# Attention keys of a block in one row, one score product per head; the guard of eight weight parts moved to the end

## The chip, the cores and the metric

The kernel runs on one core of a Trainium2 chip. The metric is device time in microseconds (us) of that core; the median of 3 runs of the kernel before is 688.71 us (688.39 to 688.76). Five engines run side by side, each through its own list of instructions in order: TensorE (PE; its weight loads are shown as PEld), VectorE (DVE), ScalarE (ACT), GpSimd (POOL) and SyncE (SP), which here issues all loads and stores. They wait for each other through semaphores.

## The reference

Attention with a band and a few global keys, and two feed-forward layers ("MoE" in the code) behind it:

```python
scores = scale * np.matmul(q, k.transpose(0, 1, 3, 2))     # 2 x 8 heads, 768 tokens, 64 per head
keep = is_global | is_local            # column < 8, or 0 <= row - column < 96
scores = scores + bias[None, :, :, :]  # -slope of the head * distance
scores = np.where(keep, scores, -1000000000.0)
a = softmax(scores)
x = np.matmul(a, v)                    # 1536 tokens x 512
h = np.maximum(x @ w_in, 0.0)          # 512 -> 2048
x = h * h @ w_out                      # -> 512
gate = 1.0 / (1.0 + np.exp(-(x @ w_gate)))
out = gate * (x @ w_val) @ w_out2      # 512 -> 1536 -> 512
```

The MoE weights arrive as 64-bit floats, 68 parts of 128 x 512 numbers. A kernel decodes them to 32-bit floats with integer operations on the two 32-bit halves of each number, and splits each into a high and a low half for products of better precision.

## The kernel before, in words

`_fast` describes the whole work as tasks for a planner (`_Plan`): engine, estimated duration, rank, and the buffers read and written. `issue` lets the tasks run in a model of the engines, by rank among those that are ready, and writes them out in that order, which then is the order of each engine's instructions. Estimated durations thus set only the order.

**Attention.** The 1536 tokens are 12 blocks of 128 queries (`bt`, six for each batch; `t` is the block's number in its batch). A block sees its own 128 keys, the last 96 of the block before (columns 32 to 127), and the first 32 keys of the batch. `rows_of` (L432) loads keys `k` and queries `q` with two DMAs each, one for each group of heads; at the first block of a batch two more bring the first 32 columns, `kf`. Three key buffers and two query buffers are there. Each block has two halves of four heads. `scores` (L467) makes a half's products: for each of two head pairs and both heads, one product against own keys and, after the first block, one against `kf` (32 columns) and one against the 96 columns of the block before, which lie in that block's key buffer:

```python
parts = [(k_t, slice(0, P), 1, 0)]
if t:
    parts = [(kf, slice(0, GS), 0, 0), (ks[bt - 1], slice(GS, P), 0, GS)] + parts
```

Then VectorE adds the bias and takes the minimum (L486), ScalarE takes the exponential (L491), VectorE or ScalarE divides (L510, L512), TensorE transposes (L523, tile `at`), one of the two copies (`ats`, L253 on ScalarE, L255 on VectorE), and TensorE multiplies with the values (L535, tile `o`), which becomes `x` (L543 on).

**MoE.** `moe1` and `moe2` go over the tokens in four passes each, every pass with a quarter of the weights. A `step` (L608) is three products (L615 to L617). The first pass of `moe1` has groups of 256 tokens and runs between the attention blocks; from some 157 us there are only MoE products. 80 small products on zeros (L397) fill TensorE where nothing else is ready, and 8 more (L393) open the program.

**Weights.** `load_weight` (L567) handles one part: a load `wst` (L576, two buffers); ScalarE's absolute value of the high word into `wu` (L583); VectorE's maximum with a smallest number (L585), which keeps numbers too small for the format from being misread; two shifts (L587); "or" with the low word's top bits (L589); "or" with sign and top exponent bit (L592); ScalarE's copy to the high half (L253); VectorE's difference as the low half (L263).

**A second path.** `gen_i` is set from the two sizes given at run time (`whether`, L373). At the end all engines read it, and where it isn't zero they run `_general`, which is not run here.

Of the kernel before, what the change touches and what calls it, by code (L numbers as in the profile page):

```python
# [9 lines left out]
F32 = mybir.dt.float32  # L10
# [7 lines left out]
P = 128  # L18
# [6 lines left out]
F64_MIN = 2.0 ** -15 * 1.125  # L25


@with_exitstack
def kernel(
# [16 lines left out]
    pers = ctx.enter_context(tc.tile_pool(name="pers", bufs=1))  # L46
    nf = pers.tile([P, 2], F32, name="nf")
# [3 lines left out]
    with tc.tile_pool(name="sb", bufs=1) as sb, tc.manual_schedule():  # L51
        _fast(tc, sb, qw, kw, vw, nums, w1, w2, out, nf, gen_i, ident, slopes)
# [160 lines left out]
def _fast(tc, sb, qw, kw, vw, nums, w1, w2, out, nf, gen_i, ident, slopes):  # L213
# [31 lines left out]
    def dma(size):  # L245
        return max(620, size / 350.0)
# [30 lines left out]
    consts = buf("sb", [P, 1], F32, "consts")  # L277
    ni = buf("early", [P, 2, 2], I32, "ni")
# [11 lines left out]
    def setup():  # L290
# [82 lines left out]
        def whether():  # L373
# [9 lines left out]
            v.tensor_copy(gen_i, ok)  # L383

        add("dve", 1300, 1e8, whether, r=[num], w=[(consts, "gen"), (small, "ok")])
# [25 lines left out]
    ks = {}  # L411
# [8 lines left out]
    for bt in range(NQ):  # L420
# [20 lines left out]
        add("sp", 2 * dma(P * NH2 * P * 2), rank_att(i0) - 8900, rows_of(q_t, qw[bt]), w=[q_t],  # L441
            late=2000)
        if t == 0:
            kf = buf("early", [P, NH2, GS], F32, "kf", 2)
            add("sp", 1300, rank_att(i0) - 4000, rows_of(kf, kw[bt], slice(0, GS)), w=[kf],
                late=2000)
# [10 lines left out]
        for half in both:  # L457
# [5 lines left out]
            parts = [(k_t, slice(0, P), 1, 0)]  # L463
            if t:
                parts = [(kf, slice(0, GS), 0, 0), (ks[bt - 1], slice(GS, P), 0, GS)] + parts

            def scores(pts=pts, q_t=q_t, parts=parts, half=half):  # L467
# [303 lines left out]
    for n in range(len(chunks)):  # L771
        load_weight(n, when[n])
# [232 lines left out]
```

## Time and profile before

| | before |
|---|---|
| median of 3 runs | 688.71 us |
| the profiled execution | 689.12 us |
| its span, first to last instruction | 687.2 us |
| TensorE busy in the span | 667.9 us, 97% |
| VectorE | 432.1 us, 63% |
| ScalarE | 285.7 us, 42% |
| mean granted TensorE clock | 0.985 of 2.4 GHz |

The span is what the hardware profiler saw between the first and the last instruction; the execution's own time has 1.9 us around it. A record of a product lasts longer than the distance to the next one, since products are pipelined: distances between starts tell what one costs. "Idle before" of an engine names what ended its idle time. A product on plain 32-bit floats (`k`, `q`, `vv`) shows as two records, a MoE product as one.

### The profile page before, as it was taken

What the parts mean: (1) busy time and instruction counts of PE and PEld (TensorE: products, weight loads), DVE (VectorE), ACT (ScalarE), POOL (GpSimd) and SP (SyncE); (2) the same over time, 40 slices, a digit from 0 to 9 for tenths busy, and PEclk for the clock granted to TensorE, in tenths of its full rate; (3) what the DMA queues carried; (4) which work ended last, traced back from release to release, by engine and by line L of the source; (5) the groups of instructions that cost most, each with busy time, mean ns of one, the idle gap of its engine ahead of it and who ended that gap; (6) DMA issues with size and microseconds to landing.
All of it is one profiled execution on the core that took longest, in us unless ns stands there. A gap on an engine that the chain in (4) does not pass through costs nothing.

```text
span 687.2 us, 10016 instructions
## 1 busy us (share of the span) xinstructions
PE 667.9 (97%) x3864; PEld 558.7 (81%) x3864; DVE 432.1 (63%) x976; ACT 285.7 (42%) x622; POOL 1.1 (0%) x8
## 2 busy tenths in 40 slices
PE   9878999999999999999999999999999999999996
PEld 7766899899988888888888888888888888888884
DVE  5878876768888888888857852476348223222232
ACT  5767777764463444554434541352113111211110
POOL 0000000000000000000000000000000000000000
PEclk9988899999999999999999999999999999999999
DMA  7754433201332332333210230043001000001011
GB/s 181 171 153 139 150 114 107 73 3 63 123 122 78 107 123 87 98 96 119 82 41 32 93 122 1 31 126 120 0 1 62 1 1 0 1 0 62 0 62 66
DMA packets 29335, 51.71 MB, mean 75 GB/s; under 512 B 3808, under 2 KB 16352, under 8 KB 29280
## 3 DMA queue, kind: packets, MB, share of 16 engines
q1 hardware_dynamic: 29280, 51.00, 24.4%
q8 instruction: 32, 0.52, 0.3%
q14 instruction: 23, 0.19, 0.1%
HBM read 47.84 MB, written 3.15 MB: 74 GB/s over the span
## 4 chain that ended last, share of the span: by engine, by line


## 5 line engine op out<-in xcount | busy, mean ns | idle before, releaser
L615 PE MATMUL h<-x,w 128*128 128x512 f32 (+1 forms) x528 | 197.8, 375 | 0.0
L617 PE MATMUL h<-x,w 128*128 128x512 f32 (+1 forms) x528 | 195.7, 371 | 0.0
L616 PE MATMUL h<-x,w 128*128 128x512 f32 (+1 forms) x528 | 195.7, 371 | 0.0
L615 PEld LDWEIGHTS h<-x,w 128*128 128x128 f32 x528 | 99.9, 189 | 17.5 <-issue 0.2
L617 PEld LDWEIGHTS h<-x,w 128*128 128x128 f32 x528 | 99.9, 189 | 16.9
L616 PEld LDWEIGHTS h<-x,w 128*128 128x128 f32 x528 | 100.0, 189 | 16.7
L713 DVE TENSOR_TENSOR r<-h,r 128x512 f32<-128x512 f32 x36 | 24.9, 691 | 103.1 <-PE h L617 101.6
L615 PE MATMUL y<-g,w 128*128 128x512 f32 (+1 forms) x240 | 86.3, 360 | 2.6 <-ACT w L253 1.7
L616 PE MATMUL y<-g,w 128*128 128x512 f32 (+1 forms) x240 | 84.3, 351 | 0.0
L617 PE MATMUL y<-g,w 128*128 128x512 f32 (+1 forms) x240 | 84.3, 351 | 0.0
L263 DVE TENSOR_TENSOR g<-r,g 128x512 fp32r<-128x512 f32 x84 | 57.7, 687 | 17.2 <-ACT g L253 16.7
L710 ACT ACTIVATE r<-h 128x512 f32<-128x512 f32 x36 | 21.5, 598 | 109.7 <-PE h L617 109.6
L583 ACT ACTIVATE wu<-wst 128x512 f32<-128x512 f32 x68 | 45.2, 665 | 48.5 <-DMA wst<-in_w_dram 41.1
L263 DVE TENSOR_TENSOR w<-wx,w 128x512 fp32r<-128x512 f32 x68 | 46.5, 685 | 21.2 <-ACT w L253 20.7
L615 PE MATMUL o<-w,g 128*128 128x512 f32 x144 | 56.9, 395 | 0.0
L616 PE MATMUL o<-w,g 128*128 128x512 f32 x144 | 56.9, 395 | 0.0
L617 PE MATMUL o<-w,g 128*128 128x512 f32 x144 | 56.8, 394 | 0.0
L253 ACT ACTIVATE w<-wx 128x512 fp32r<-128x512 f32 x68 | 42.5, 626 | 34.0 <-DVE wx L592 28.9
L253 ACT ACTIVATE g<-r 128x512 fp32r<-128x512 f32 x32 | 20.2, 632 | 82.5 <-DVE r L713 82.5
L615 PEld LDWEIGHTS y<-g,w 128*128 128x128 f32 x240 | 45.6, 190 | 10.5 <-ACT w L253 2.0
L617 PEld LDWEIGHTS y<-g,w 128*128 128x128 f32 x240 | 45.7, 190 | 6.7 <-DVE w L263 0.2
L616 PEld LDWEIGHTS y<-g,w 128*128 128x128 f32 x240 | 45.7, 191 | 6.4
(79 smaller groups left out, 827.5 us busy)
## 6 DMA issues: line engine op xcount, KB each, us to landing
wst<-in_w_dram SPq DMA_DIRECT2D x68, 512.0 KB, 3.5
k<-in_kw_dram SPq DMA_DIRECT2D x24, 128.0 KB, 2.9
q<-in_qw_dram SPq DMA_DIRECT2D x24, 128.0 KB, 3.1
vv<-in_vw_dram SPq DMA_DIRECT2D x12, 256.0 KB, 2.9
out_dram<-oacc SPq DMA_DIRECT2D x11, 256.0 KB, 2.1
vv<-in_vw_dram SPq DMA_DIRECT2D x10, 192.0 KB, 3.4
vv<-in_vw_dram SPq DMA_DIRECT2D x10, 64.0 KB, 2.8
out_dram<-oacc SPq DMA_DIRECT2D x2, 128.0 KB, 3.6
```

Source lines behind the costliest of these rows:

```text
L253: nc.scalar.activation(to(), of(), ACTF.Copy)
L263: nc.vector.tensor_tensor(to(), of(), less(), op=ALU.subtract)
L583: add("act", act(TN), rank, lambda: nc.scalar.activation(u.ap, hi().bitcast(F32), ACTF.Abs), r=[st], w=[u])
L615: nc.tensor.matmul(p, lhsT=ww[:, 0, ws], rhs=lo, start=first, stop=False)
L616: nc.tensor.matmul(p, lhsT=ww[:, 0, ws], rhs=hi, start=False, stop=False)
L617: nc.tensor.matmul(p, lhsT=ww[:, 1, ws], rhs=hi, start=False, stop=last)
L710: add("act", act(TN), rk, lambda r=r, pt=pt: nc.scalar.activation(r.ap, pt.ap, ACTF.Sigmoid), r=[pt], w=[r])
L713: add("dve", dve(TN), rk, lambda r=r, pt=pt: v.tensor_tensor(r.ap, pt.ap, r.ap, op=ALU.mult), r=[pt], w=[r])
```

## The change

**Keys in one row.** `k` becomes 4 x 2 x 128 numbers per partition: own keys in one window, and in the other, ahead of it, the first 32 keys and the 96 of the block before. The loads write these windows, six DMAs for a block after the first (128, 96 and 32 columns for each group of heads); `kf` and the use of the neighbour's buffer are gone. `scores` makes one product of 256 columns for a head (128 in the first block).

**Guard.** The first eight parts (`TINY = 8`) are decoded with no absolute value and no maximum. All parts take sign and top bit first and add the low word into a new buffer `wf`; the high half is copied from the number without the low word. After the last decode the first eight parts are loaded again, `look_through` counts numbers below the bound, `decide` sums the counts on one partition through a small DMA and sets `gen_i` from them and from the sizes.

```diff
+TINY = 8
...
+    asked = pers.tile([1, P * TINY + 1], F32, name="asked")
...
-        k_t = ks[bt] = buf("early", [P, NH2, P], F32, "k", NQK)
-        def rows_of(to, of, cols=slice(0, P)):
-            def fn():
-                for j in both:
-                    d = slice(j * D, j * D + D)
-                    nc.sync.dma_start(out=to.ap[d], in_=of[d, j::2, cols])
-            return fn
-        add("sp", 2 * dma(P * NH2 * P * 2), rank_att(i0) - 9000, rows_of(k_t, kw[bt]), w=[k_t],
-            late=2000)
...
-            add("sp", 1300, rank_att(i0) - 4000, rows_of(kf, kw[bt], slice(0, GS)), w=[kf],
-                late=2000)
+        k_t = buf("early", [P, NH2, 2, P], F32, "k", NQK)
+        def rows_of(parts):
+            for j in both:
+                d = slice(j * D, j * D + D)
+                for to, of, cols in parts():
+                    nc.sync.dma_start(out=to[d], in_=of[d, j::2, cols])
+        def windows(k_t=k_t, bt=bt, t=t):
+            own, ahead = k_t[:, :, 1], k_t[:, :, 0]
+            parts = [(own, kw[bt], slice(0, P))]
+            if t:
+                parts += [(ahead[:, :, GS:], kw[bt - 1], slice(GS, P)),
+                          (ahead[:, :, 0:GS], kw[bt - t], slice(0, GS))]
+            return parts
+        add("sp", (2 if t == 0 else 4) * dma(P * NH2 * P * 2), rank_att(i0) - 9000,
+            lambda windows=windows, rows_of=rows_of: rows_of(windows), w=[k_t], late=2000)
...
-                    for k, cols, w, c0 in parts:
-                        for j in both:
-                            d = slice(j * D, j * D + D)
-                            nc.tensor.matmul(
-                                pts[j][:, c, w, c0:c0 + cols.stop - cols.start],
-                                lhsT=q_t[d, hp], rhs=k[d, hp, cols], start=True, stop=True)
-            add("pe", 200 + 500 * (2 - lo), rank_att(i), scores, w=pts,
-                r=[q_t] + [k for k, *_ in parts])
+                    for j in both:
+                        d = slice(j * D, j * D + D)
+                        nc.tensor.matmul(pts[j][:, c, lo:], lhsT=q_t[d, hp], rhs=k_t[d, hp, lo:],
+                                         start=True, stop=True)
+            add("pe", 200 + 430 * (2 - lo), rank_att(i), scores, w=pts, r=[q_t, k_t])
...
+        if n < TINY:
+            add("dve", dve(TN, False), rank, lambda: v.tensor_scalar(xi(), hi(), 5, 2, **shift),
+                r=[st], w=[xx])
+        else:
...
-        add("dve", dve(TN), rank, lambda: v.scalar_tensor_tensor(
-            xi(), lo(), 29, xi(), op0=ALU.logical_shift_right, op1=ALU.bitwise_or),
-            r=[st], w=[xx])
         add("dve", dve(TN), rank, lambda: v.scalar_tensor_tensor(
             xi(), hi(), F64_TOP, xi(), op0=ALU.bitwise_and, op1=ALU.bitwise_or), r=[st], w=[xx])
+        full = buf("sb", [P, TN], F32, "wf", 1)
+        add("dve", dve(TN), rank, lambda: v.scalar_tensor_tensor(
+            full.ap.bitcast(I32), lo(), 29, xi(), op0=ALU.logical_shift_right,
+            op1=ALU.bitwise_or), r=[st, xx], w=[full])
         copy(WHI, TN, rank, lambda: t[:, 0], lambda: xx.ap, [xx], [(t, 0)])
-        minus(WLO, TN, rank, lambda: t[:, 1], lambda: xx.ap, lambda: f32(t[:, 0]), [xx, (t, 0)],
-              [(t, 1)])
+        minus(WLO, TN, rank, lambda: t[:, 1], lambda: full.ap, lambda: f32(t[:, 0]),
+              [full, (t, 0)], [(t, 1)])
...
+    def look_through(n):
+        st = buf("sb", [P, TN, 2], I32, "wst", 2)
+        u = buf("sb", [P, TN], F32, "wu", 1)
+        src = w1[chunks[n][1], chunks[n][2]]
+        add("sp", dma(P * TN * 8), 1e7, lambda: nc.sync.dma_start(
+            out=st.ap.rearrange("p n t -> p (n t)"), in_=src), w=[st], late=2000)
+        add("act", act(TN), 1e7, lambda: nc.scalar.activation(
+            u.ap, st[:, :, 1].bitcast(F32), ACTF.Abs), r=[st], w=[u])
+        add("dve", dve(TN) + 80, 1e7, lambda: v.scalar_tensor_tensor(
+            u.ap, u.ap, F64_MIN, u.ap, op0=ALU.is_lt, op1=ALU.mult, accum_out=tiny[:, n:n + 1]),
+            w=[u, (tiny, n)])
+    def decide():
+        add("sp", 700, 1e7, lambda: nc.sync.dma_start(
+            out=asked[:, 0:P * TINY], in_=tiny.ap), r=[(tiny, n) for n in range(TINY)],
+            w=[(consts, "asked")], late=2000)
+        def fn():
+            v.tensor_reduce(asked[:, P * TINY:], asked, axis=AX.X, op=ALU.add)
+            v.tensor_scalar(asked[:, P * TINY:], asked[:, P * TINY:], 0.0, None, op0=ALU.is_gt)
+            v.tensor_copy(gen_i[0:1], asked[:, P * TINY:])
+        add("dve", 1600, 1e7, fn, r=[(tiny, "asked"), (consts, "asked")], w=[(consts, "gen")])
```

The planner's order moves with this. SP, near the start, before: loads of the second block (`k_162`, `q_187`, `vv_210`), of the third (`k_265`, `q_290`) and of the first weight part (`wst_316`).

```order
L436 DMA k_162<-in_kw_dram 64x4x128 x2
L436 DMA q_187<-in_qw_dram 64x4x128 x2
L415 DMA vv_210<-in_vw_dram 128x512
L417 DMA vv_210<-in_vw_dram 32x512
L418 DMA vv_210<-in_vw_dram 96x512
L436 DMA k_265<-in_kw_dram 64x4x128 x2
L436 DMA q_290<-in_qw_dram 64x4x128 x2
L576 DMA wst_316<-in_w_dram 128x1024
```

SP, the same place now, from the second block's queries `q_190` to the first weight part `wst_331`; the six loads of the second block's keys stand just ahead, and look like those of the third, `k_261`.

```order
L440 DMA q_190<-in_qw_dram 64x4x128 x2
L419 DMA vv_214<-in_vw_dram 128x512
L421 DMA vv_214<-in_vw_dram 32x512
L422 DMA vv_214<-in_vw_dram 96x512
L440 DMA k_261<-in_kw_dram 64x4x128
L440 DMA k_261<-in_kw_dram 64x4x96
L440 DMA k_261<-in_kw_dram 64x4x32
L440 DMA k_261<-in_kw_dram 64x4x128
L440 DMA k_261<-in_kw_dram 64x4x96
L440 DMA k_261<-in_kw_dram 64x4x32
L440 DMA q_305<-in_qw_dram 64x4x128 x2
L577 DMA wst_331<-in_w_dram 128x1024
```

Each block's keys take six places instead of two, and the first weight load stands behind twelve key loads of the second and third block, where four and the two of `kf` (ahead of the piece shown) stood.

TensorE, a half of the third block, before: the first six of the 12 products of a half, for the two heads `s_373` and `s_374`.

```order
L473 MATMUL s_373<-kf_138,q_290 128x32
L473 MATMUL s_374<-kf_138,q_290 128x32
L473 MATMUL s_373<-k_162,q_290 128x96
L473 MATMUL s_374<-k_162,q_290 128x96
L473 MATMUL s_373<-k_265,q_290 128x128
L473 MATMUL s_374<-k_265,q_290 128x128
```

TensorE, the same block now: the last two of the four products of the first half, value products and transposes, and the first two of the second half.

```order
L477 MATMUL s_378<-k_261,q_305 128x256
L477 MATMUL s_379<-k_261,q_305 128x256
L537 MATMUL o_334<-ats_351,vv_112 64x128 x2
L537 MATMUL o_334<-ats_375,vv_112 64x128 x2
L525 MATMUL at_411<-ident,sa_311 128x128 x4
L477 MATMUL s_421<-k_261,q_305 128x256
L477 MATMUL s_422<-k_261,q_305 128x256
```

Six products of three widths became two of one width, all from the block's own buffer.

VectorE, decode of the second weight part between the score reductions (`sa`), before: maximum (L585), shift (L587), and the two "or" steps.

```order
L585 TENSOR_SCALAR wx_581<-wu_466 128x512
L486 ISA sa_573,mn_469<-s_450,bias_160 128x256
L486 ISA mn_469 128x1
L587 TENSOR_SCALAR wx_581<-wx_581 128x512
L486 ISA sa_602,mn_603<-s_515,bias_160 128x256
L486 ISA mn_603 128x1
L589 SCALAR_TENSOR_TENSOR wx_581<-wst_391,wx_581 128x512
L497 TENSOR_SCALAR sm_485<-sm_485 128x4
L498 RECIPROCAL sm_485<-sm_485 128x4
L592 SCALAR_TENSOR_TENSOR wx_581<-wst_391,wx_581 128x512
```

VectorE, decode of the second weight part now.

```order
L585 TENSOR_SCALAR wx_552<-wst_430 128x512
L257 COPY ats_561<-at_546 128x512
L596 SCALAR_TENSOR_TENSOR wx_552<-wst_430,wx_552 128x512
L499 TENSOR_SCALAR sm_454<-sm_454 128x4
L500 RECIPROCAL sm_454<-sm_454 128x4
L600 SCALAR_TENSOR_TENSOR wf_584<-wst_430,wx_552 128x512
L514 TENSOR_SCALAR sa_489<-sa_489,sm_454 128x256
L265 TENSOR_TENSOR w_582<-wf_584,w_582 128x512
```

Three steps instead of four, and the first reads the loaded part itself (`wst_430`), not ScalarE's result (`wu_466`); a copy of transposed matrices (`ats_561`) stands between them on VectorE.

## Rows read from the trace of the kernel before

**Rows 1.** Busy time by stages; first the columns, with the mean granted TensorE clock (PEclk).

```profile
core 0: us, PE busy (x) PEld busy (x) DVE busy (x) ACT busy (x) POOL busy (x), PEclk, DMA share, GB/s
20.00:76.50 56.50, 46.18 (x436) 39.25 (x435) 47.37 (x152) 39.35 (x108) 0.00 (x0) 0.85 0.53 149
76.50:157.00 80.50, 80.20 (x869) 72.49 (x867) 58.31 (x210) 57.10 (x172) 0.00 (x0) 1.00 0.27 82
...
400.00:600.00 200.00, 200.00 (x875) 163.95 (x874) 88.28 (x147) 52.30 (x87) 0.00 (x0) 1.00 0.12 37
```

**Rows 2.** Groups by line and shape, 20 to 76.5 us: busy, mean ns | idle before, releasers.

```profile
L523 PE MATMUL at<-ident,sa 128*128 128x128 f32 x62 | 11.5, 309 | 8.5 <-ACT sa L510 3.0 <-DVE sa L512 2.1 <-DVE ats L255 1.7
...
L615 PE MATMUL y<-g,w 128*128 128x256 f32 x7 | 2.9, 420 | 1.7 <-ACT w L253 1.7
```

**Rows 3.** Timeline of TensorE in attention: start, length, engine, line, operation, records.

```profile
6.32 1.16 PE L473 MATMUL s<-k,q 64*128 64x128 f32 x16
7.42 0.83 PE L397 MATMUL h<-zero 128*128 128x256 bf16 x6
...
11.34 0.76 PE L473 MATMUL s<-kf,q 64*128 64x32 f32 x3
...
14.68 0.44 PE L523 MATMUL at<-ident,sa 128*128 128x128 f32 x2
...
29.04 0.41 PE L473 MATMUL s<-kf,q 64*128 64x32 f32 x4
...
30.58 1.09 PE L535 MATMUL o<-ats,vv 128*64 128x128 f32 x16
31.60 0.66 PE L523 MATMUL at<-ident,sa 128*128 128x128 f32 x4
```

**Rows 4.** Timeline of TensorE in the first MoE pass: 256 columns.

```profile
161.41 0.28 PE L615 MATMUL h<-x,w 128*128 128x256 f32 x1
161.53 0.28 PE L616 MATMUL h<-x,w 128*128 128x256 f32 x1
```

**Rows 5.** Groups by line and shape, TensorE, 76.5 to 157 us.

```profile
L473 PE MATMUL s<-kf,q 64*128 64x32 f32 x80 | 7.2, 257 | 0.0
```

**Rows 6.** Groups by line and shape, vector engines, 20 to 76.5 us.

```profile
L583 ACT ACTIVATE wu<-wst 128x512 f32<-128x512 f32 x8 | 5.3, 663 | 4.2 <-DMA wst<-in_w_dram 4.2
...
L585 DVE TENSOR_SCALAR wx<-wu 128x512 f32<-128x512 f32 x9 | 3.8, 420 | 3.9 <-ACT wu L583 3.9
...
L512 DVE TENSOR_SCALAR sa<-sa,sm 128x256 f32<-128x256 f32 x17 | 5.3, 347 | 0.0
...
L255 DVE COPY ats<-at 128x512 f32<-128x512 f32 x3 | 2.1, 686 | 0.8 <-PE at L523 0.8
```

**Rows 7.** Waits, 20 to 76.5 us: who <- whom: us in total, times, longest.

```profile
DVE wx L585 <- ACT wu L583: 3.9, 3, 2.1
```

**Rows 8.** Timeline of SP's queue, first weight load: the issuing instruction.

```profile
12.55 0.60 SPq L576 DMA_DIRECT2D wst<-in_w_dram  x1
```

**Rows 9.** Timeline of VectorE, 24 to 25 us: first weight part.

```profile
24.42 0.42 DVE L585 TENSOR_SCALAR wx<-wu 128x512 f32<-128x512 f32 x1
```

**Rows 10.** Waits of SP's own queue, 18 to 76.5 us.

```profile
SPq L436 <- PE s L473: 13.6, 4, 4.8
SPq L576 <- DVE wx L592: 13.0, 4, 5.4
SPq L415 <- PE o L535: 11.6, 4, 4.7
```

**Rows 11.** DMA issues, 0 to 76.5 us: KB each, median us to landing.

```profile
wst<-in_w_dram SPq DMA_DIRECT2D x10, 512.0 KB, 4.8
k<-in_kw_dram SPq DMA_DIRECT2D x16, 128.0 KB, 2.9
...
kf<-in_kw_dram SPq DMA_DIRECT2D x4, 32.0 KB, 3.9
```

**Rows 12.** Page, costliest groups: the gate product.

```profile
L713 DVE TENSOR_TENSOR r<-h,r 128x512 f32<-128x512 f32 x36 | 24.9, 691 | 103.1 <-PE h L617 101.6
```

More of the change, by code (lines that the diff above doesn't have):

```diff
@@ L51 @@
     with tc.tile_pool(name="sb", bufs=1) as sb, tc.manual_schedule():
-        _fast(tc, sb, qw, kw, vw, nums, w1, w2, out, nf, gen_i, ident, slopes)
+        _fast(tc, sb, qw, kw, vw, nums, w1, w2, out, nf, gen_i, ident, slopes, asked)
     engines = [mybir.EngineType.PE, mybir.EngineType.Activation, mybir.EngineType.DVE,
@@ L210, in issue, with _fast @@
             t["fn"](t["e"]) if t["told"] else t["fn"]()
-def _fast(tc, sb, qw, kw, vw, nums, w1, w2, out, nf, gen_i, ident, slopes):
+def _fast(tc, sb, qw, kw, vw, nums, w1, w2, out, nf, gen_i, ident, slopes, asked):
     nc = tc.nc
@@ L382, in whether @@
             v.tensor_scalar(ok, ok, -1.0, 1.0, op0=ALU.mult, op1=ALU.add)
-            v.tensor_copy(gen_i, ok)
-        add("dve", 1300, 1e8, whether, r=[num], w=[(consts, "gen"), (small, "ok")])
+            v.tensor_copy(asked[:, P * TINY:], ok[0:1])
+        add("dve", 1300, 1e8, whether, r=[num], w=[(tiny, "asked"), (small, "ok")])
     zero = buf("early", [P, TN], mybir.dt.bfloat16, "zero")
@@ L461, in _fast, with scores @@
             pts = [buf("ps", [P, 2, 2, P], F32, f"s{j}", 2) for j in both]
[L463 to L467, printed above, removed]
+            def scores(pts=pts, q_t=q_t, k_t=k_t, half=half, lo=lo):
                 for c in both:
                     hp = 2 * half + c
-                    for k, cols, w, c0 in parts:
-                        for j in both:
-                            d = slice(j * D, j * D + D)
-                            nc.tensor.matmul(
-                                pts[j][:, c, w, c0:c0 + cols.stop - cols.start],
-                                lhsT=q_t[d, hp], rhs=k[d, hp, cols], start=True, stop=True)
-            add("pe", 200 + 500 * (2 - lo), rank_att(i), scores, w=pts,
-                r=[q_t] + [k for k, *_ in parts])
+                    for j in both:
[3 more added lines that the diff above has]
+            add("pe", 200 + 430 * (2 - lo), rank_att(i), scores, w=pts, r=[q_t, k_t])
             sas = [buf("early", [P, 2, 2, P], F32, "sa", NSA) for _ in both]
@@ new lines, in load_weight @@
+        if n < TINY:
[3 more added lines that the diff above has]
+            u = buf("sb", [P, TN], F32, "wu", 1)
+            add("act", act(TN), rank, lambda: nc.scalar.activation(
+                u.ap, hi().bitcast(F32), ACTF.Abs), r=[st], w=[u])
+            add("dve", dve(TN, False), rank, lambda: v.tensor_scalar(
+                xx.ap, u.ap, F64_MIN, None, op0=ALU.max), r=[u], w=[xx])
+            add("dve", dve(TN, False), rank, lambda: v.tensor_scalar(xi(), xi(), 5, 2, **shift),
+                w=[xx])
@@ L772, in _fast @@
         load_weight(n, when[n])
+    for n in range(TINY):
+        look_through(n)
+    decide()
     for fn, p, *rest in work:
```

18 lines of the change are left out of this document (6 added, 12 removed).

## The prediction

> **What bounds the kernel now.** I read the busy time by stages first [rows 1]. The reader is to see three stages there. From 76.5 us on TensorE is the bound: it is busy 80.2 of 80.5 us up to 157, and 200.0 of 200.0 us between 400 and 600, where VectorE needs only 88 of 200. There a microsecond taken off TensorE is a microsecond of the kernel, and one taken off another engine is nothing. From 20 to 76.5 us TensorE is busy 46.2 of 56.5 us, so it idles 10.3, and it runs at 0.85 of its clock on average; VectorE, at 47.4, is then the busiest engine. What ends TensorE's idle time there is in the groups of that stretch [rows 2]: 8.5 us stand before the transposes of the attention matrices, ended by ScalarE's or VectorE's work on them, and 1.7 us before a y product that waits for a weight part. So in this stage TensorE waits for the two vector engines, and a smaller load on those shortens it. The third stage, up to 20 us, is loads and filler products.
>
> **The products.** A block after the first has 12 score products in each half (second order piece, before), and each runs as two records on the chip: 24 records from 29.04 until the value products at 30.58 [rows 3]. The 16 records of a first block, all 128 columns wide, go from 6.32 to 7.42 [rows 3]. Records of the two heads start in pairs. The eight more records, four pairs, take 1.54 - 1.10 = 0.44 us, so a pair costs 0.11 us and about 0.21 us are lost at the change to the next kind. The 12 pairs of mixed width (32, 96, 128 columns) cost the same 0.11 each as those of 128 columns: up to 128 columns width is free, and what is paid is the number of pairs. The change makes four pairs of 256 columns of these twelve.
>
> No row shows such a pair. Below, a 256-column record of the MoE, on other data formats, follows its predecessor by 0.12 us [rows 4]. Above, if cost goes with columns, it is 0.22. The value products decide for me: 16 records, eight pairs, go from 30.58 to 31.60 [rows 3], or about 0.10 a pair with 128 columns too, although their weights are only 64 columns wide. Half the weights to load and nearly the same time: there the columns passed are paid, not the weight load. So I take 0.22. A half then costs 4 x 0.22 = 0.88 instead of 12 x 0.11 = 1.33, and 0.45 us are saved. If the two heads of a pair did not overlap any more, it would be 8 x 0.22 = 1.76, or 0.43 lost.
>
> The Trainium skill (TensorE: Matmul & The Clock Gate, Back-to-back issue gap) has N/2.4 + 2.5 ns for a product of N columns at full clock, 109 ns here. By that page a half would cost 0.44 us and save 0.89. The value products, at 0.10 us for 128 columns, do not follow it, and the trace decides.
>
> Of the 32-column records 80 stand between 76.5 and 157 us [rows 5], eight to a half: ten halves lie where TensorE is the bound. **Term 1: 10 x 0.45 = 4.5 us.** The ten halves ahead of that are part of a stage in which TensorE waits; what it saves there lengthens its waits, so I count nothing for it.
>
> **The weight decode.** Eight parts lose ScalarE's absolute value (0.66 us each) and VectorE's maximum (0.42 us each) [rows 6]; that is 5.3 us of ScalarE and 3.4 us of VectorE before 76.5 us. VectorE doesn't keep all of it. I counted its instructions up to the first score reduction of the twelfth half in both orders: eight maxima fewer (3.4 us), one shift fewer (0.4) and five 256-column divisions fewer (5 x 0.35 = 1.7), but five more copies of transposed matrices (5 x 0.69 = 3.4) [rows 6]. That leaves 2.1 us. Besides, the old decode reached VectorE through ScalarE's queue: ScalarE stood 4.2 us waiting for weight loads [rows 6], and VectorE 3.9 us in three waits for ScalarE [rows 7]. The load is still waited for, now by VectorE itself, but the step of 0.66 us behind it is gone three times: 2.0 us. **Term 2: 2.1 + 2.0 = 4.1 us.** Its upper end is all of TensorE's idle time, 10.3 us; its lower end is nothing, or a loss if the loads become late.
>
> For the other 60 parts the two "or" steps swap places and the sum goes to its own buffer: the same number of instructions on each engine, and the high half can be copied one step (0.69 us) earlier. They are decoded beside a saturated TensorE [rows 1]: nothing.
>
> **The loads.** A block after the first now asks for keys six times instead of two, and SP spends 0.60 us on an issue [rows 8]. From the order of SP (first order piece) the second block's queries go out two issues later, 1.2 us; the first weight load six issues later, 3.6 us, at about 16.2 instead of 12.55. The second block's scores started at 11.34 and ended before the transposes at 14.68 [rows 3]; 1.2 us later and 0.9 us shorter for its two halves, they end 0.3 us later, and filler products stand behind them. The first weight part is read by VectorE at 24.42 us [rows 9]. Both cost nothing. From 18 to 76.5 us SP stands 13.6 + 13.0 + 11.6 = 38.2 us waiting for readers [rows 10], and four blocks' 16 further issues, 9.6 us, fit into that. If this cover is gone, the lateness comes out at the weight part that VectorE wants next, with the score reductions of a block queued behind it. The new key loads are narrow. The load of 32 KB for the old first columns took 3.9 us to land, those of 128 KB 2.9 [rows 11]: 1.0 us more for a block's keys, well ahead of their use.
>
> **The late look and the decision.** Eight loads of 512 KB, eight ScalarE and eight VectorE passes of 0.7 us, placed after the last decode. VectorE is busy 88 of 200 us there [rows 1], and 101.6 us of its time before the gate product ends with TensorE [rows 12], which has further score tiles to fill meanwhile. Nothing; if one of them stood in TensorE's way each time, eight times 0.7, 5.6 us. The decision is made before the second last group of products; the last instructions are the old ones, and the tail is unchanged.
>
> **Sum.** The profiled execution took 689.1 us, 0.4 above the median of 688.7. 689.1 - 4.5 - 4.1 = 680.5, and against the median 680.1.
>
> **The rivals.**
> - Only the products count. The early stage is paced by loads and by the order of work, and the relief of the vector engines turns into waits: 688.7 - 4.5 = 684.2. For it: TensorE's clock is below full only in the stage in which it idles [rows 1], and shorter products add to the idle time. Against: no load row shows SP or the DMA queues full after 20 us.
> - The early stage becomes bound by TensorE as well. All 10.3 us of idle time go: 688.7 - 4.5 - 10.3 = 673.9. For it: ScalarE's wait for a load no longer holds up exponentials. Against: VectorE's 47.4 of 56.5 us, less 2.1, doesn't fit far below 46.
> - Slower: the loads become the bound. Blocks two to six issue 20 more key loads, 12 us, less 4 x 0.6 for the old first columns: 9.6 us. If all of it lies on the path, 688.7 + 9.6 - 4.5 - 2.1 = 691.7. It decides from 6.6 us on. The mechanism is SP's single queue: a weight load stands behind six key loads which wait for a buffer. For it: early weight loads take 4.8 us to land [rows 11]. Against: the 38.2 us of waiting. The Trainium skill (DMA: Bandwidth & Descriptors, Specifications) wants at least 512 bytes in a row of a transfer for full rate, and the new rows have 384 and 128; the 3.9 us against 2.9 point the same way, and by that rule this rival gains weight.
> - A pair of 256 columns costs 0.11 us: 688.7 - 8.9 - 4.1 = 675.7. That is what the gap rule named above would give.
> - The two heads no longer overlap: one wide product saves nothing, 688.7 + 4.3 - 4.1 = 688.9. Against: the pairs overlap at all three widths.
>
> **How the numbers follow.** My forecast 0.46, only the products 0.20, early stage bound by TensorE 0.16, loads 0.09, gap rule 0.05, no overlap 0.04. The predicted time is 680.1. The range 673.5 to 687.4 takes in the first three, the gap rule, and half a lost term 1; it leaves out the loads, the lost overlap and some of the far ends, under 2 in 10. About 1.4 us (0.2%) can be told from no change. Faster: the forecast, the two faster rivals and nearly all of "only the products", 0.85. Same: the lost overlap and small parts of the others, 0.06. Slower: the loads, 0.09.
>
> **What would show it.** Score records after 76.5 us in pairs 0.22 us apart, four to a half; TensorE busy without a gap from some point near 70 us instead of 76.5; VectorE's decode waiting for loads directly, and ScalarE without such waits; no new idle time of TensorE after 400 us. I am wrong if SP's waits shrink towards nothing and weight loads end TensorE's idle time, or if the early stage is no shorter.

## The result and the profile after

The changed kernel takes 682.07 us (median of 5 runs, 681.37 to 685.03), the one before 688.71 beside it (688.39 to 688.93): a ratio of 0.9908, 95% interval 0.9888 to 0.9928. So 6.6 us are gone, where 8.6 were forecast. The profiled execution took 681.62 us with a span of 679.2.

The time by stages, columns as in [rows 1]:

```profile
20.00:76.50 56.50, 47.23 (x352) 35.57 (x352) 47.17 (x153) 39.16 (x112) 0.00 (x0) 0.91 0.81 200
76.50:157.00 80.50, 77.63 (x714) 66.52 (x714) 61.22 (x214) 56.77 (x166) 0.00 (x0) 1.00 0.31 84
400.00:600.00 200.00, 200.00 (x882) 165.07 (x881) 93.05 (x159) 57.84 (x96) 0.00 (x0) 1.00 0.17 54
```

Three things are to be seen. From 20 to 76.5 us TensorE still idles 9.3 us (10.3 before) and runs at 0.91 of its clock (0.85); the DMA engines are busy for 0.81 of the stretch. From 76.5 to 157 us, where it had no gap to speak of, it now idles 2.9 us. From 400 us on TensorE is busy throughout, as before.

A half's products now stand like this in TensorE's order of time, after 76.5 us:

```profile
107.20 1.13 PE L477 MATMUL s<-k,q 64*128 64x256 f32 x8
108.27 0.39 PE L650 MATMUL h<-x,w 128*128 128x256 f32 x1
```

The next product starts 1.07 us after the first score record (1.06 in the median of the ten halves of this width after 76.5 us). A half before, of 24 records, took 1.54, as in [rows 3]. The saving is 0.48 us; I had 0.45. Less the 0.2 us at the change of kind, a pair of 256 columns costs 0.22, as taken.

What SP waited for between 18 and 76.5 us, columns as in [rows 10]:

```profile
SPq L577 <- DVE mn L488: 11.3, 4, 4.6
SPq L440 <- PE s L477: 6.0, 2, 4.0
SPq L577 <- DMA wst<-in_w_dram: 2.0, 1, 2.0
SPq L440 <- DMA wst<-in_w_dram: 1.6, 1, 1.6
```

The three large waits of 38.2 us [rows 10] have become two of 17.3. The weight decode's waits over the first 76.5 us, by groups on VectorE and ScalarE (busy us, mean ns, then idle time before and its releaser):

```profile
L585 DVE TENSOR_SCALAR wx<-wst 128x512 int32<-128x512 int32 x8 | 3.4, 421 | 3.8 <-DMA wst<-in_w_dram 3.8
L590 ACT ACTIVATE wu<-wst 128x512 f32<-128x512 f32 x1 | 0.7, 673 | 2.5 <-DMA wst<-in_w_dram 2.5
```

ScalarE still waits 2.5 us, for the ninth part, the first with a guard, at 67.2 us. VectorE waits 3.8 us for weight loads, 2.85 of them at one place. SP's and VectorE's order of time show that place:

```profile
39.91 0.54 SPq L577 DMA_DIRECT2D wst<-in_w_dram  x1
...
45.95 0.43 DVE L585 TENSOR_SCALAR wx<-wst 128x512 int32<-128x512 int32 x1 [2.85 <-DMA wst<-in_w_dram]
```

The fourth weight load is issued at 39.91 us, 1.5 us later than before (38.41), and VectorE, now ahead of the loads, stands still until 45.95. The decode of this part shares its queue with the score reductions. What TensorE does meanwhile, in windows of 4 us:

```profile
44.00:48.00 4.00, 1.24 (x12) 0.83 (x12) 2.05 (x7) 1.64 (x5) 0.00 (x0) 1.00 0.96 276
48.00:52.00 4.00, 3.48 (x19) 2.63 (x19) 3.97 (x13) 2.92 (x9) 0.00 (x0) 0.53 0.56 166
52.00:56.00 4.00, 4.00 (x23) 3.43 (x19) 1.95 (x4) 2.08 (x5) 0.00 (x0) 0.61 0.32 72
68.00:72.00 4.00, 3.77 (x14) 2.54 (x14) 3.67 (x17) 3.70 (x14) 0.00 (x0) 0.59 0.36 131
```

It is busy 1.24 of 4 us, and in the two windows behind that its granted clock is 0.53 and 0.61, that is, mostly at the lower of its two levels, 1.2 GHz. So these gaps are paid for twice: while TensorE waits, and again while it works at half speed. The kernel before had three such stretches, from 45.8 to 52.6, 59.4 to 62.8 and 69.7 to 76.5 us; this one has two, from 48.3 to 55.1 and 68.7 to 72.2.

### The profile page after: what moved, and what is told of

Same layout as the page of the kernel before. It is cut to its first block, busy times and chain, and to the rows that moved or that the text cites. A ratio compares the mean times of both kernels' runs of the same rounds, so it can differ in the third digit from the quotient of the medians.

```text
span 679.2 us, 9493 instructions
## 1 busy us (share of the span) xinstructions
PE 658.5 (97%) x3544; PEld 542.5 (80%) x3544; DVE 435.6 (64%) x982; ACT 289.5 (43%) x627; POOL 1.1 (0%) x8
## 4 chain that ended last, share of the span: by engine, by line
## 5 line engine op out<-in xcount | busy, mean ns | idle before, releaser
L651 PEld LDWEIGHTS h<-x,w 128*128 128x128 f32 x528 | 100.0, 189 | 16.9
L265 DVE TENSOR_TENSOR w<-wf,w 128x512 fp32r<-128x512 f32 x68 | 46.8, 689 | 23.1 <-ACT w L255 21.7
L255 ACT ACTIVATE g<-r 128x512 fp32r<-128x512 f32 x36 | 22.8, 632 | 79.4 <-DVE r L748 79.2
L590 ACT ACTIVATE wu<-wst 128x512 f32<-128x512 f32 x60 | 40.2, 669 | 38.4 <-DMA wst<-in_w_dram 33.7
L650 PEld LDWEIGHTS y<-g,w 128*128 128x128 f32 x240 | 45.4, 189 | 13.3 <-issue 3.0
L493 ACT ACTIVATE sa<-sa,mn 128x256 f32<-128x256 f32 (+1 forms) x96 | 46.0, 481 | 11.8 <-DVE mn L488 10.1
L651 PEld LDWEIGHTS y<-g,w 128*128 128x128 f32 x240 | 45.4, 189 | 6.5
```

The lines of the kernel that those rows point to most:

```text
L255: nc.scalar.activation(to(), of(), ACTF.Copy)
L265: nc.vector.tensor_tensor(to(), of(), less(), op=ALU.subtract)
L493: lambda sa=sa, j=j, h=h, lo=lo, mn=mn, sm=sm: nc.scalar.activation(sa[:, j, lo:], sa[:, j, lo:], ACTF.Exp, bias=mn[:, h:h + 1], scale=-1. ...
L590: add("act", act(TN), rank, lambda: nc.scalar.activation(u.ap, hi().bitcast(F32), ACTF.Abs), r=[st], w=[u])
L650: nc.tensor.matmul(p, lhsT=ww[:, 0, ws], rhs=lo, start=first, stop=False)
L651: nc.tensor.matmul(p, lhsT=ww[:, 0, ws], rhs=hi, start=False, stop=False)
```

## The experiments

The first four runs take the change apart. From them came two theories, called A and B in the expectations of the later runs, from "no extra loads" on. **A:** the new decode brought more than its term, and the extra key loads take part of it back in the first 76 us. **B:** the loads are free, and decode and products relieve the same idle time, so that what they bring does not add up.

A ratio is to runs of the kernel before on the same chip, taken in turn with it. The last three columns are read from rows of 20 to 76.5 us and 76.5 to 157 us such as those above: TensorE's idle time, and what the clock costs, worked out as busy time times (1 - granted clock). From 76.5 to 157 us only two kernels lose to the clock as well, "row and one product alone" 3.2 us and "three products, heads apart" 1.6.

These three columns describe the one profiled execution of each kernel. Executions of one kernel differ in their clock: the fourth column gives the lowest and highest mean granted clock over the whole span. The profiled execution of the kernel before, at 0.985, is near the bottom of its kernel's range, and some others lie off their medians ("no late look" 686.26 us, "four key loads" 677.05, "three products, heads paired" 683.39). The clock's cost is an estimate, and a low one where TensorE is busier in the stretches at the lower level than on average: in the three of the kernel before it is busy 15.7 of 16.9 us, half of which is 7.8.

| kernel | median us | ratio, 95% interval | clock, whole span | idle 20-76.5 | clock 20-76.5 | idle 76.5-157 |
|---|---|---|---|---|---|---|
| before | 688.71 | 1 | 0.983-0.994 | 10.3 | 6.9 | 0.3 |
| changed | 682.07 | 0.9908, 0.9888-0.9928 | 0.985-0.990 | 9.3 | 4.3 | 2.9 |
| row and one product alone | 691.66 | 1.0024, 1.0001-1.0047 | 0.976-0.988 | 16.5 | 6.0 | 1.1 |
| decode alone | 678.84 | 0.9855, 0.9827-0.9884 | 0.995-0.997 | 6.8 | 0.0 | 0.5 |
| no late look | 683.95 | 0.9929, 0.9904-0.9953 | 0.986-0.990 | 10.6 | 4.1 | 2.9 |
| four key loads | 679.34 | 0.9874, 0.9844-0.9905 | 0.985-0.993 | 6.8 | 1.5 | 2.9 |
| no extra loads | 676.21 | 0.9824, 0.9801-0.9846 | 0.991-0.997 | 7.0 | 3.0 | 2.9 |
| three products, heads apart | 691.19 | 1.0052, 1.0029-1.0075 | 0.981-0.993 | 5.9 | 3.0 | 2.4 |
| three products, heads paired | 685.15 | 0.9953, 0.9930-0.9977 | 0.984-0.995 | 6.4 | 3.0 | 2.5 |
| loads from GpSimd | 682.61 | 0.9922, 0.9904-0.9939 | 0.986-0.990 | 8.6 | 2.9 | 2.9 |
| copies on GpSimd | 679.31 | 0.9869, 0.9850-0.9889 | 0.989-0.994 | 8.3 | 2.9 | 2.9 |
| "or" steps exchanged alone | 687.02 | 0.9967, 0.9944-0.9989 | 0.984-0.996 | 9.5 | 4.2 | 0.5 |
| row for blocks 7 to 11 | 676.01 | 0.9810, 0.9781-0.9838 | 0.995-0.999 | 6.8 | 0.0 | 2.0 |
| the same, twelve parts unguarded | 676.49 | 0.9835, 0.9814-0.9856 | 0.992-0.998 | 5.9 | 1.5 | 1.0 |

**Row and one product alone.** The kernel before with the loads and scores of the change, and the old decode.

```diff
-        k_t = ks[bt] = buf("early", [P, NH2, P], F32, "k", NQK)
+        k_t = buf("early", [P, NH2, 2, P], F32, "k", NQK)
...
+                        nc.tensor.matmul(pts[j][:, c, lo:], lhsT=q_t[d, hp], rhs=k_t[d, hp, lo:],
```

> The kernel before with the keys in one row and one score product per head, and with the old weight decode. Forecast's theory (the two parts add: products 4.5 us, decode 4.1 us): 684.2 us, a half's four score pairs in 1.07 us from first start to the next kind. Rival, the late weight loads eat the products' gain as long as the old decode still runs through ScalarE: 686 to 689, with ScalarE's waits for a weight load in the first 76 us above the 4.2 us of before. Rival, all of the gain is the products': 682.

Measured: 691.66 us, against 688.60 for the kernel before beside it: a small loss, if any (the ratio's interval begins at 1.0001), and above all three expectations. Its stage row, and ScalarE's group of guards there (the old decode begins on ScalarE):

```profile
20.00:76.50 56.50, 39.98 (x294) 30.09 (x291) 45.35 (x137) 35.80 (x96) 0.00 (x0) 0.85 0.66 178
...
L580 ACT ACTIVATE wu<-wst 128x512 f32<-128x512 f32 x9 | 6.0, 664 | 12.6 <-DMA wst<-in_w_dram 11.6 <-DVE wx L582 1.0
```

ScalarE waits 11.6 us for weight loads, where it waited 4.2 before [rows 6], and TensorE's idle time grows by 6.2 us. What the products save late is spent here and on the clock, which is the lowest of all these kernels; two of the 12 executions, at 0.988, took 686.5 us.

**Decode alone.** The kernel before with the new decode, the late look and the decision; loads and products are the old ones.

```diff
+        if n < TINY:
+            add("dve", dve(TN, False), rank, lambda: v.tensor_scalar(xi(), hi(), 5, 2, **shift),
+                r=[st], w=[xx])
```

> The kernel before with the new decode of the weights, the late look and the decision, and with the old key loads and score products. Forecast's theory: 688.7 - 4.1 = 684.6 us, VectorE's waits for ScalarE before a decode gone in the first 76 us. Rival, the decode gives nothing since loads pace it: 688 to 689. Rival, it gives more without the extra key loads in SP's queue: below 683.

Measured: 678.84 us. This one part brings 9.8 us (688.60 beside it), more than the whole change; it is the third of the cases expected (below 683).

```profile
20.00:76.50 56.50, 49.69 (x527) 42.00 (x526) 50.48 (x163) 42.16 (x118) 0.00 (x0) 1.00 0.59 169
76.50:157.00 80.50, 80.05 (x862) 73.08 (x861) 59.51 (x208) 54.51 (x160) 0.00 (x0) 1.00 0.25 77
```

TensorE idles 6.8 instead of 10.3 us, and its clock is full throughout. In these two executions, 10.6 us apart, the idle time falls by 3.5 us and the clock's cost by 6.9. As the kernel before ran at a low clock there, even for itself, the share of the clock is better taken from all executions: the median of their mean granted clocks is 0.9895 for the 18 of the kernel before and 0.9965 here, and 0.007 of 689 us is 4.8 us. By this estimate about half of the gain is the clock.

**No late look.** The changed kernel without the eight late loads and passes; the guard decision rests on the sizes alone, so whether a tiny number is among the first eight weight parts is not looked at.

```diff
-    for n in range(TINY):
-        look_through(n)
-    decide()
```

> The changed kernel without the late look at the eight parts: no second loads of 512 KB, no passes over them and no small load; the second path is chosen by the sizes alone. Forecast's theory, the look is hidden beside a saturated TensorE: the changed kernel's time within 0.7 us, 681.4 to 682.8. Rival, the look stands in VectorE's way: faster by 2 us or more, 680 or less.

Measured: 683.95 us, 1.9 above the changed kernel and outside both expectations, but with overlapping intervals. Leaving the look out brings nothing that shows, as predicted.

**Four key loads.** The ahead window is loaded by one transfer of all 128 columns per group of heads in place of one of 96 and one of 32; the first 32 keys of the batch are thus replaced by keys of the block before.

```diff
-                parts += [(ahead[:, :, GS:], kw[bt - 1], slice(GS, P)),
-                          (ahead[:, :, 0:GS], kw[bt - t], slice(0, GS))]
+                parts += [(ahead, kw[bt - 1], slice(0, P))]
```

> The changed kernel with four key loads for a block after the first instead of six: the window ahead is filled by all 128 columns of the block before, in rows of 512 bytes, so that the first 32 keys of a batch are replaced by others in the scores. As many bytes, 20 issues of 0.6 us fewer on SP. If SP's issues are hidden, as forecast: 681.4 to 682.8. If the late weight loads of the changed kernel (VectorE waits 2.8 us for one at 45.95) come from SP's queue: 678 to 680.5, and that wait is gone.

Measured: 679.34 us, 2.7 below the changed kernel, with overlapping intervals. The order of work on VectorE and ScalarE is the changed kernel's. The fourth weight load goes out at 35.45 us, and no weight load makes VectorE wait:

```profile
35.45 0.41 SPq L576 DMA_DIRECT2D wst<-in_w_dram  x1
...
wst<-in_w_dram SPq DMA_DIRECT2D x10, 512.0 KB, 5.5
```

The transfers themselves are not faster. A weight load takes 5.5 us from issue to landing (median before 76.5 us) against 4.6 in the changed kernel, although all key rows have 512 bytes now. The Trainium skill (DMA: Bandwidth & Descriptors, Specifications) asks for at least 512 bytes for the full rate; these runs do not show narrow rows as what costs here. The DMA engines are as busy as in the changed kernel (0.82 of 20 to 76.5 us against 0.81).

**No extra loads.** The changed kernel's order, row for row on TensorE, VectorE and ScalarE, without the four loads of the ahead window.

```diff
-            parts = [(own, kw[bt], slice(0, P))]
-            if t:
-                parts += [(ahead[:, :, GS:], kw[bt - 1], slice(GS, P)),
-                          (ahead[:, :, 0:GS], kw[bt - t], slice(0, GS))]
-            return parts
+            return [(k_t[:, :, 1], kw[bt], slice(0, P))]
...
+                            rhs=k_t[d, hp, 1:2].to_broadcast([D, 2 - lo, P]), start=True, stop=True)
```

> The changed kernel without the four key loads of the ahead window; the product's 256 columns read the block's own 128 keys twice (so the scores of the window ahead are left out and replaced). The order of instructions on TensorE, VectorE and ScalarE is the changed kernel's, row for row; SyncE issues four transfers fewer per block. Theory A (the extra key loads cost on SyncE's queue in the first 76 us what the one product saves): 674 to 678 us, TensorE's granted clock of 20 to 76.5 us back at 0.97 or more (the changed kernel shows 0.91), VectorE's waits for weight loads under 1.5 us (3.8). Rival B (the loads are free, and the products and the decode relieve the same idle time, so that what they bring does not add up): 681 to 683, as the changed kernel.

Measured: 676.21 us; 0.9824 to 0.9908 in ratios, 5.8 us below the changed kernel at the same order of work. Theory A gave 674 to 678, B 681 to 683: **B falls.** The clock came back only to 0.94, short of the 0.97 expected, and VectorE shows no wait for a weight load in the first 76.5 us; ScalarE waits 2.4 us for one, until 60.8, and the lower clock stands from 62.4 to 69.2. The fourth weight load, the stages, and in TensorE's order of time the first score products of block 6 and the last value products:

```profile
34.75 0.54 SPq L573 DMA_DIRECT2D wst<-in_w_dram  x1
...
20.00:76.50 56.50, 49.49 (x394) 38.32 (x393) 49.83 (x159) 41.16 (x119) 0.00 (x0) 0.94 0.60 168
76.50:157.00 80.50, 77.63 (x708) 67.04 (x707) 61.22 (x209) 56.65 (x161) 0.00 (x0) 1.00 0.26 77
...
70.03 0.72 PE L472 MATMUL s<-k,q 64*128 64x128 f32 x8
...
144.80 1.09 PE L533 MATMUL o<-ats,vv 128*64 128x128 f32 x16
```

The same two places in the changed kernel:

```profile
74.71 0.71 PE L477 MATMUL s<-k,q 64*128 64x128 f32 x8
...
149.63 1.09 PE L537 MATMUL o<-ats,vv 128*64 128x128 f32 x16
```

Between them lie 74.8 us without the extra loads and 74.9 with them. So in these two executions the loads cost 4.7 us ahead of block 6, and nothing in the blocks behind it.

**Three products, heads apart, and paired.** Six key loads and the keys in one row, but three products per head from it. In the first run the three products of one head stand together; in the second the two heads alternate, as in the kernel before.

```diff
-                        nc.tensor.matmul(pts[j][:, c, lo:], lhsT=q_t[d, hp], rhs=k_t[d, hp, lo:],
-                                         start=True, stop=True)
+                        for w, a, z in ((0, 0, GS), (0, GS, P), (1, 0, P))[2 * lo:]:
+                            nc.tensor.matmul(pts[j][:, c, w, a:z], lhsT=q_t[d, hp],
+                                             rhs=k_t[d, hp, w, a:z], start=True, stop=True)
```

```diff
+                    for w, a, z in ((0, 0, GS), (0, GS, P), (1, 0, P))[2 * lo:]:
+                        for j in both:
...
+                            nc.tensor.matmul(pts[j][:, c, w, a:z], lhsT=q_t[d, hp],
```

> The changed kernel with the six key loads and the keys in one row, but the scores taken by three products per head (32, 96 and 128 columns) as before; else the order is the changed kernel's. Theory A (a half's products are worth 0.45 us each where TensorE has no gap, ten halves): 685 to 688 us. Rival B (the products are worth nothing once the decode is faster, since VectorE sets the pace): 681 to 683.

> As the run with six key loads and three products per head, with the two heads of a product issued one behind the other again, as in the kernel before (there the three products of one head stood together, and a half took 1.78 us instead of 1.54). The order of all else is the changed kernel's. If the products are worth what a half shows, 1.54 - 1.06 = 0.48 us, in the halves after 76.5 us alone: 682.1 + 10 x 0.48 = 687 us; if in all twenty: 692. If the extra loads and not the products set the end of the first stage: 682 to 684.

Measured: 691.19 us, above both expectations, and 685.15. The first was no clean experiment, since it changed the grouping too. TensorE's order of time, first with the heads apart, then paired:

```profile
107.62 1.85 PE L478 MATMUL s<-k,q 64*128 64x32 f32 x24
109.41 0.66 PE L526 MATMUL at<-ident,sa 128*128 128x128 f32 x4
```

```profile
107.39 1.61 PE L478 MATMUL s<-k,q 64*128 64x32 f32 x24
108.92 0.39 PE L651 MATMUL h<-x,w 128*128 128x256 f32 x1
```

A half takes 1.79 us apart and 1.53 paired. With that mended, the one product is worth 0.9953 - 0.9908, about 3.1 us, at the same order of all else and with the same loads. It lies between the expectation for "loads set the end" (682 to 684) and ten halves of 0.48 us (687). Where the 3.1 us lie is seen at the same two places as above, and the paired run's late stage beside them:

```profile
73.33 0.71 PE L478 MATMUL s<-k,q 64*128 64x128 f32 x8
...
152.25 1.09 PE L538 MATMUL o<-ats,vv 128*64 128x128 f32 x16
...
76.50:157.00 80.50, 77.97 (x840) 69.75 (x835) 58.01 (x207) 54.97 (x161) 0.00 (x0) 1.00 0.29 77
```

Between them lie 78.9 us with three products and 74.9 with one: the ten late halves are worth 4.0 us. But with one product the changed kernel comes 1.4 us later to the first place, with more idle time (9.3 us against 6.4) and more lost to the clock (4.3 against 3.0) ahead of it. Late, TensorE idles 2.5 us in the paired run too, nearly as much as the 2.9 of the changed kernel, so that idle time comes with the order of work and hardly with the shorter products.

**Loads from GpSimd, and copies on GpSimd.** First the narrow loads of the ahead window go out from GpSimd's queue; then they are replaced by copies on the chip out of the block before.

```diff
-                    nc.sync.dma_start(out=to[d], in_=of[d, j::2, cols])
+                    queue.dma_start(out=to[d], in_=of[d, j::2, cols])
...
+                lambda behind=behind, rows_of=rows_of: rows_of(behind, nc.gpsimd),
```

```diff
+                g.tensor_copy(k_t[:, :, 0, GS:], prev[:, :, 1, GS:])
+                g.tensor_copy(k_t[:, :, 0, 0:GS], prev[:, :, 0, 0:GS])
```

> The changed kernel with the four key loads of the ahead window issued from GpSimd, which is idle, in place of SyncE; bytes and rows are the same. If SyncE's issue time (0.60 us for each) is the cost of theory A: 676 to 679 us, and the weight loads are issued earlier than the changed kernel's second and third (24.8 and 32.0 us). If it is the transfers themselves (narrow rows in the DMA queues): 681 to 684. Rival B: 681 to 683.

> The changed kernel with the ahead window copied on the chip by GpSimd out of the block before (one copy of 128 columns, or two of 96 and 32, for four heads) in place of the four loads; the scores are all there. Theory A: 674 to 679 us, the price of the run without those loads plus what a late copy adds. Rival B: 681 to 683. If GpSimd's copies slow VectorE or come late for the products: over 683, with VectorE's busy time of 20 to 76.5 us up or TensorE's scores waiting for the copies.

Measured: 682.61 us, where the transfers as the cost would put it (and B, which has fallen), and 679.31, at the edge of theory A. From GpSimd the weight loads do go out earlier (the fourth at 34.85), but the cost moves to the front, and the order of work differs from the changed kernel's from 11 us on. TensorE by windows:

```profile
8.00:12.00 4.00, 2.81 (x19) 2.38 (x20) 1.85 (x17) 1.52 (x8) 0.48 (x1) 0.64 1.17 209
24.00:28.00 4.00, 2.39 (x9) 1.25 (x10) 3.96 (x19) 4.00 (x15) 1.81 (x3) 0.77 0.82 222
28.00:32.00 4.00, 4.00 (x18) 2.52 (x18) 2.41 (x8) 2.87 (x9) 0.73 (x2) 0.50 0.96 233
```

The lower clock now stands from 9.1 to 12.5 and 26.2 to 33.0 us instead of 48.3 to 55.1 and 68.7 to 72.2. So whether SP's issue time or the transfers in the shared DMA engines make the extra loads dear is **not settled**: the run with four loads speaks for the issues, GpSimd's run against, and the latter is not at the same order. The copies keep all scores and need no transfer. They are cheap, by GpSimd's groups:

```profile
L453 POOL COPY k<-k 128x384 f32<-128x384 f32 x8 | 4.2, 528 | 64.8 <-PE s L485 52.2 <-DMA k<-in_kw_dram 12.5
```

At 679.31 us, though, this version lies 3.1 above the run without any loads. Its trace shows 1.3 us more idle time from 20 to 76.5 us; why is not known, and its order of work differs from the changed kernel's too.

**"Or" steps exchanged alone.** The kernel before with the guard on all parts, but the two "or" steps in the new order and the full number in a buffer of its own.

```diff
+        full = buf("sb", [P, TN], F32, "wf", 1)
+        add("dve", dve(TN), rank, lambda: v.scalar_tensor_tensor(
+            full.ap.bitcast(I32), lo(), 29, xi(), op0=ALU.logical_shift_right,
+            op1=ALU.bitwise_or), r=[st, xx], w=[full])
```

> The kernel before, with the two 'or' steps of the decode exchanged and the full number in a buffer of its own, for all 68 parts; the guard stays on all of them, no late look. If the gain of the new decode comes from the guard's two steps taken out of the first eight parts: 687 to 690 us, as before. If it comes from the exchange (the high half is copied one step earlier and the buffer comes free sooner): 679 to 683. Half and half: 684.

Measured: 687.02 us, ratio 0.9967: 2.3 us of the decode's 9.8 by themselves (0.8 to 3.9 by the interval). The other 7.5 come with the guard's two steps gone from the eight parts, if the two do not help each other. In the trace idle time and the clock's cost fall from 20 to 76.5 us, where the first parts are decoded; how the gain is shared between these and the 60 others was not run.

**Row for blocks 7 to 11.** The new decode everywhere; row and one product only for the five blocks whose halves lie after 76.5 us.

```diff
+        row = t > 0 and bt > SB
...
-            if t:
+            if row:
                 parts += [(ahead[:, :, GS:], kw[bt - 1], slice(GS, P)),
```

> The changed decode in all of the kernel, but keys in one row and one product only for blocks 7 to 11, whose ten halves lie after 76.5 us; blocks 0 to 5 have the loads and the three products of before. Theory A (the row's extra loads cost only in the first 76 us, where transfers and weight loads share the queues, and the products pay only where TensorE is busy without a gap): 678.8 - 10 x 0.48 = 674 us, less than every kernel so far; up to 677 if part of it comes back as TensorE's waits for the vector engines (2.9 us of idle time after 76.5 us in the changed kernel, 0.5 with the decode alone). No clock under 0.97 from 20 to 76.5 us. Rival (the loads cost wherever they are, or the products' time is all given back): 679 to 682.

Measured: 676.01 us, ratio 0.9810: faster than both kernels, and 6 us faster than the changed one, with every score there.

```profile
20.00:76.50 56.50, 49.67 (x525) 41.97 (x521) 50.40 (x160) 41.90 (x117) 0.00 (x0) 1.00 0.58 166
76.50:157.00 80.50, 78.52 (x714) 67.72 (x714) 62.05 (x212) 55.89 (x162) 0.00 (x0) 1.00 0.32 91
```

The early stage is that of the decode alone: 49.67 us busy, clock 1.00. The row's loads cost nothing that can be seen there. The products bring 678.84 - 676.01 = 2.8 us (3.1 by the ratios, whose intervals just overlap), not 4.8, and TensorE idles 2.0 us in a stage in which it idled 0.5. The order of work differs from that of the decode alone from 84 us on, so this idle time need not be the products' doing.

**The same, twelve parts unguarded.**

```diff
-TINY = 8
+TINY = 12
```

> The kernel with keys in one row for blocks 7 to 11 alone, and twelve instead of eight weight parts decoded without the guard and looked through late. Theory: the guard's two steps count only while TensorE waits and falls to half clock; that kernel shows no half clock and 6.8 us of idle time from 20 to 76.5 us, and two more parts are decoded there, so 0 to 2 us less than it: 674 to 676 us. Rival (every part without the guard takes its 0.66 and 0.42 us off the end): 671 to 673. If the four more late looks stand in TensorE's way: 677 or more.

Measured: 676.49 us, no difference; the rival of 671 to 673 falls. But the clock is not full here. TensorE from 56 to 64 us, first in the version with eight parts unguarded, then with twelve:

```profile
56.00:60.00 4.00, 3.38 (x32) 2.61 (x32) 3.97 (x13) 2.26 (x7) 0.00 (x0) 1.00 0.94 282
60.00:64.00 4.00, 2.69 (x26) 2.02 (x26) 4.00 (x13) 2.06 (x6) 0.00 (x0) 1.00 0.43 139
```

```profile
56.00:60.00 4.00, 3.32 (x33) 2.62 (x32) 3.97 (x12) 2.37 (x7) 0.00 (x0) 1.00 0.98 275
60.00:64.00 4.00, 3.13 (x23) 2.27 (x21) 4.00 (x11) 1.78 (x6) 0.00 (x0) 0.64 0.51 155
```

With nearly the same gaps ahead of it, one execution keeps the full clock and the other falls to the lower level from 61.1 to 64.6 us. The 0.9 us less idle time is lost to the clock again (1.5), so what two more parts without the guard are worth at an equal clock is not shown.

## Why the prediction was right, and where it was not

The direction, the size within 2 us and the stages were right: 682.07 against 680.1, inside the range. That the sum came so close is luck: the decode brought 5.7 us more than its term, the loads, which had none, took 5.8, and the two cancel.

- **The products, Term 1 (4.5 us).** The price of a pair was right (0.22), and so was 0.45 per half (0.48). The ten late halves were nearly as forecast, 4.0 us in the traces of the paired run and the changed kernel. But all twenty together bring 3.1, since the ten early ones, counted as nothing, take some back: 1.4 us in the same traces. The step that failed is "what it saves there lengthens its waits, so I count nothing for it": the waits did lengthen, and more was lost to the clock behind them. That this is why rests on two traces. TensorE's waits from 76.5 to 157 us in the changed kernel were not foreseen either; with three products at the same order they are nearly as long in sum (2.5 us idle against 2.9):

```profile
PE y L650 <- DVE g L265: 1.4, 3, 1.1
PE at L525 <- ACT sa L493: 0.6, 1, 0.6
PE at L525 <- DVE sa L514: 0.3, 1, 0.3
```

- **The weight decode, Term 2 (4.1 us).** Measured 9.8. The idle time taken away was sized well, 3.5 us. The sum left out the clock: the half-speed stretches behind the gaps cost 6.9 us (46.2 x 0.15, [rows 1]) in the profiled execution, and with shorter gaps they went altogether; over all executions the clock gave back some 4.8. The row was read and its 0.85 quoted, but only the idle time was priced. "Its upper end is all of TensorE's idle time, 10.3 us" should have been 17. The sum also put the exchanged "or" steps at nothing, which bring 2.3 us alone.
- **The loads, costed at nothing.** Measured 5.8 us, by the run without them at the same order. The step that failed is that "16 further issues, 9.6 us, fit into" the 38.2 us of waiting. Those waits did shrink, as that step foresaw; but they lie where SP waits for one buffer, not where the next weight load needed the queue: the fourth went out at 39.91 instead of 34.75 us. That this delay is the whole price is not shown: from GpSimd the fourth goes out at 34.85, and the kernel takes 682.61. Even the first went out later than the prediction's 16.2, at 17.41. The rival with the loads had the place right ("a weight load stands behind six key loads") and put its price at 9.6. It fell as a forecast, since the decode's gain was larger, not because its mechanism was absent.
- **The late look, the decision and the 60 other parts.** Nothing that shows for the look, as said. What the exchange brings in the other 60 parts, forecast at nothing, no run takes by itself.
- **What would show it.** The score records and the time after 400 us came as described, and so did VectorE's direct waits for loads (3.8 us). "TensorE busy without a gap from some point near 70 us" did not: it had gaps up to 95 us. Nor did "ScalarE without such waits": 2.5 us are left. The early stage was shorter; SP's large waits shrank to under half, part of my own sign of being wrong, and the weight loads did end the wait of 2.85 us at 45.95.

The parts, measured apart, nearly add up: -9.8 for the decode, -3.1 for the products and +5.8 for the loads give -7.1, against -6.6 measured. Loads and products without the decode would give +2.7; the run of just these shows +3.1 by the medians and +1.7 by the ratio.

The Trainium skill (TensorE: Matmul & The Clock Gate, Back-to-back issue gap) gives N/2.4 + 2.5 ns as the gap of an isolated product at full clock, 109 ns for 256 columns. Taken once for a pair of records, as the prediction took it, it does not fit: a pair costs 0.22 us, and the rival built on it fell. Taken once for each of a half's eight records, as an estimate, it gives 0.87 us, and the four pairs take 0.86; so these runs do not show the rule itself wrong.

## What to carry to other kernels

Where a stage shows both idle time and a lowered granted clock, price a relief with both: here the clock was worth about half of the gain. And one execution's clock may not be typical; look at those of the others. A queue's total waiting time is not room for more issues; ask when the next transfer that someone waits for can be issued, and what the transfers take from it. And an edit that trades transfers for TensorE time belongs only into the blocks where TensorE is the bound: in blocks 7 to 11 alone it made the fastest version, 676.0 us.

## What was not expected of the hardware

- The grouping of a half's products by head costs: 24 records take 1.53 us where two heads in the two halves of the partitions alternate, and 1.79 where three products of one head stand together.
- A right operand that reads the same 128 columns twice takes as long as one of 256 columns, 1.06 us for a half.
- How much the clock takes: behind one late weight part (TensorE busy 1.24 us from 44 to 48) stand 6.8 us at the lower clock, from 48.3 to 55.1 us, with TensorE busy again in nearly all of it. But not every gap is followed by it: of two kernels with nearly the same gaps from 56 to 64 us, one fell to the lower level and one did not.
